# An attention layer's gate in fewer, wider products, spread over two units; two output banks weighted in one operation

## The chip, the cores and the metric

The kernel runs on one core of a Trainium2 chip. The metric is the device time of one execution in microseconds (us). The time before is 621.62 us, the median of 3 runs that lay between 620.19 and 623.57 us.

## The reference

Three layers follow one another, all in float32:

1. Attention with a window: 4 batches, 8 heads, 576 positions, 64 features a head. A position sees itself and the 127 positions before it, with a bias that falls linearly with the distance. The result is 2304 tokens (rows) of 512 features.
2. A first mixture of 8 experts. A token's logits are `x @ w_gate` (8 columns); a ninth column, `x @ w_skip`, says whether the token takes part at all. The expert with the largest logit gets the token: `out = x + gate * relu(x @ w1[e]) @ w2[e]`.
3. A second mixture of 8 experts, in which each expert takes exactly 288 tokens, handed out in the order of the sorted logits. Its logits are 8 more columns of the rows that the first mixture leaves.

Of each finished row of attention the kernel thus needs 17 numbers: 8 logits of the first mixture, the skip score, and 8 logits of the second (which the experts' own output is added to later). In the kernel the 17 columns of weights are one tile, `wcat`, of 128 partitions by 4 chunks of features by 17.

## The kernel before

The 2304 rows are 18 tiles (`t`) of 128 rows. Attention works in **units** `u`: a tile and a half of its heads (`g` = 0 or 1, four heads each), so `u = 2t + g` runs from 0 to 35. The loop over `u` is written out by hand, and every engine executes its instructions in the order in which the code emits them. One pass of the loop holds parts of three units:

- `scores(u)`: 8 products of a query block with 192 keys into two banks of PSUM, `sa` and `sb` (line 196, PE); per head an addition of the bias with the maximum on VectorE (L206), and an exponential on ScalarE (L210), four of each.
- `attend(u - 2)`: the weighted sums over the values, 8 products of half a bank's rows (L247) and 8 of all rows (L253), into two banks `av0` and `av1`; then VectorE multiplies each bank with the reciprocal sums and writes the unit's 256 columns of the row tile `xr[t]` (L257, once for each bank).
- `probs_t(u - 1)`: the probabilities are transposed on PE (L218) and copied to SBUF, `T1` by VectorE (L226) and `T2` by ScalarE (L228).

In every second pass (`g` = 0, from u = 4 on) two more pieces stand around these:

- `gate_x(t - 2)`, ahead of `scores(u)`: the row tile of two tiles ago is transposed on PE (L398, four blocks) and copied by ScalarE to `xt` (L401).
- `gate_l(t - 2)`, behind `attend(u - 2)`: the 17 logits of its 128 rows in 16 small products of 32 rows by 17 columns (`by_quarters`, L410). VectorE copies them (L420, L421), and SP stores the rows to `x2rows` (L422).

A float32 product shows in the trace as two MATMULs and two LDWEIGHTS, so the 16 small products of a tile are 32 and 32 instructions; a transpose shows as one of each.

After a few tiles `gate_l` also appends a generator to `self.steps`: `dispatch` for four tiles (two for the last), `dispatch_one` for the tiles 14 and 15. These choose the expert and the slot of each row and scatter the rows to the experts' slots by GpSimd (POOL). A generator advances one step at each `tick()`, and two while two generators wait; the ticks stand between the VectorE operations of `scores`, `attend` and `probs_t`, nine in a unit. What is left of them is drained behind the loop. Each of them takes one PSUM buffer of the tag `gate`, of which there are two, and which `gate_x`, `gate_l`, `early_gate` and `early_turn` use too.

`early_gate` and `early_turn` (in eight units from u = 15 on) multiply the last two experts' second weights with the second mixture's gate ahead of time (L383, L391). `route_constants` makes constants and is called ahead of the loop; `search_constants` is called at u = 10. `shift_v(t)` copies a tile of values to tiles displaced by 64 rows, on POOL; `attend` reads them. `keep_warm` feeds PE products of zeros in the first microseconds.

Behind the loop come `gate_x` and the logits of tile 16, the last two units, and those of tile 17 inside `layer1`; they keep the 16 small products. `layer1` and `layer2` then run the experts. Nothing of the experts' products can start before the last tile's routing is known.

Of the kernel before, what the change touches and what calls it, by code (L numbers as in the profile page):

```python
# [8 lines left out]
F32 = mybir.dt.float32  # L9
# [3 lines left out]
AF = mybir.ActivationFunctionType  # L13
OP = mybir.AluOpType
AX = mybir.AxisListType

B, H, S, D = 4, 8, 576, 64
# [3 lines left out]
E = 8  # L21
# [17 lines left out]
WARM = (10, 4, 8)  # L39
# [11 lines left out]
class Kernel:  # L51
# [55 lines left out]
    def keep_warm(self, ps, n, name, bufs=1):  # L107

        if not n:
            return  # L110
        p = ps.tile([128, 2, D] if name[:2] == "av" else [128, 4, 128], F32, name=name, bufs=bufs)
        m = p.shape[1] * p.shape[2]
        for _ in range(n):
            self.nc.tensor.matmul(p.rearrange("p h d -> p (h d)"), self.ones, self.zeros[:, :m],
                                  start=True, stop=True)

    def mask_constants(self, pool):

# [27 lines left out]
    def attention(self, debug=None):  # L146
        tc, nc = self.tc, self.nc
# [4 lines left out]
        ps = pool("attps", 1, space=bass.MemoryType.PSUM)  # L152
# [77 lines left out]
        def attend(u):  # L230
            t, g = divmod(u, 2)
            if g == 0:
                self.xr[t] = self.tail.tile([128, SW], F32, name=f"xr{t}") if t in LAST else \
                    self.work.tile([128, SW], F32, name="xr", bufs=9)
                nc.gpsimd.iota(self.xr[t][:, XW:XW + 1], pattern=[[0, 1]], base=128 * t, channel_multiplier=1,
                               allow_small_or_imprecise_dtypes=True)
            av = [ps.tile([128, 2, D], F32, name=f"av{b}") for b in range(2)]
            own, before, mid, early, late = vt[t % NV], vt[max(t - 1, 0) % NV], vs[t % NVS], \
                vs[max(t - 1, 0) % NVS], vs[(t + 1) % NVS]


            for h in range(4):
                r = slice(64 * (h % 2), 64 * (h % 2) + 64)
                small = (own, late) if h % 2 == 0 else (early, before)
                for half in range(2):
                    m = slice(64 * half, 64 * half + 64)
                    nc.tensor.matmul(av[h % 2][m, h // 2], T2[u][r, h // 2, m], small[half][r, 4 * g + h],  # L247
                                     start=(h < 2), stop=False)
            for h in range(4):
                big = (before, mid) if h % 2 == 0 else (mid, own)  # L250
                for half in range(2):
                    m = slice(64 * half, 64 * half + 64)
                    nc.tensor.matmul(av[h % 2][m, h // 2], T1[u][:, h, m], big[half][:, 4 * g + h],  # L253
                                     start=False, stop=(h >= 2))
            x = self.xr[t][:, 256 * g:256 * g + 256].rearrange("p (h b d) -> p h b d", b=2, d=D)
            for b in range(2):
                nc.vector.tensor_tensor(x[:, :, b], av[b], rs[u][:, :, b].to_broadcast([128, 2, D]), op=OP.mult)  # L257
                self.tick()

        self.xr, self.to_slots = {}, []  # L260
# [8 lines left out]
        load_v(1)  # L269
        self.bias_kind(1, 0, 4)  # L270
        self.bias_kind(0, 0, 4)
        self.keep_warm(ps, WARM[1], "av0")
        self.bias_kind(1, 4, 8)
        self.bias_kind(0, 4, 8)
        load_v(2)
# [5 lines left out]
        def gate_l(t):  # L281
            self.gate_l(t)
            if t in ends:
                self.steps.append(self.dispatch(*ends[t]))
            if t in (NT - 4, NT - 3):
                self.steps.append(self.dispatch_one(t, self.lg[:, t]))
# [8 lines left out]
        for u in range(NU):  # L295
            t, g = divmod(u, 2)
            c = t // 2
            if u >= 4 and g == 0:
                self.gate_x(t - 2)
            scores(u)  # L300
            if not u:
                self.keep_warm(ps, WARM[2], "av0")
            if g == 0 and t + 3 < NT:
                load_v(t + 3)
            if g == 0 and t + 1 < NT:
                shift_v(t + 1)
            if u % 4 == 1 and c + 2 < NC:
                load_qk(c + 2)
            if u >= 2:
                attend(u - 2)  # L310
            if u >= 4 and g == 0:
                gate_l(t - 2)
            if u in GATES:
                i = GATES.index(u)
                (self.early_gate, self.early_turn)[i % 2](i // 2)
            if u >= 1:
                probs_t(u - 1)
            if u in LOADS:
                load_w(LOADS.index(u))
            if 3 <= u < 3 + E:  # L320
                first = N * (u - 3)
                nc.sync.dma_start(self.slots[first:first + C1].rearrange("(c n) s -> n c s", c=2),
                                  self.pad[:R1, None, :].to_broadcast([R1, 2, SW]))
            if u == 10:
                self.search_constants()
            if u in (2, 4):
                self.bias_kind(1 + u // 2, 0, 8)
# [21 lines left out]
    def route_constants(self, pool):  # L349

        nc, c = self.nc, self.consts
        self.wcat = c.tile([128, 4, 2 * E + 1], F32, name="wcat")
        nc.sync.dma_start(self.wcat, self.wcat_in)
        self.first = c.tile([128, 1, E], F32, name="first")
        nc.gpsimd.iota(self.first, pattern=[[0, 1], [-1, E]], base=E, channel_multiplier=0,
                       allow_small_or_imprecise_dtypes=True)
        self.base = c.tile([1, 1, E], BF, name="base")
        nc.gpsimd.iota(self.base, pattern=[[0, 1], [N, E]], base=0, channel_multiplier=0,
                       allow_small_or_imprecise_dtypes=True)
        self.w2g = c.tile([128, 16, E], F32, name="w2g")  # L360
        self.count2 = c.tile([128, CAP], F32, name="count2")
        self.count1 = self.count2[:, :C1]
        nc.gpsimd.iota(self.count2, pattern=[[1, CAP]], base=1, channel_multiplier=0,
                       allow_small_or_imprecise_dtypes=True)
        self.lg = c.tile([128, NT, 2 * E + 1], F32, name="lg")
        self.slot = c.tile([128, NT], I32, name="slot")
        self.seen_b = c.tile([128, 1, E], BF, name="seen_b")
        nc.gpsimd.memset(self.seen_b, 0.0)
        pad = pool.tile([128, SW], F32, name="pad")
        nc.gpsimd.memset(pad, 0.0)  # L370
        nc.gpsimd.memset(pad[:, XW:XW + 1], SKIP)
        self.pad = pad
# [32 lines left out]
    def by_quarters(self, p, x, w):  # L405

        for k in range(4):
            for j in range(4):
                m = slice(32 * j, 32 * j + 32)
                self.nc.tensor.matmul(p[m], x[:, k, m], w[:, k], start=(k == 0), stop=(k == 3))  # L410

    def gate_l(self, t):
        nc = self.nc
        p = self.gate_tile([128, 2 * E + 1])
        self.by_quarters(p, self.xt, self.wcat)
        self.keep_l(t, p)

    def keep_l(self, t, p):
# [159 lines left out]
    def layer1(self):  # L578
# [177 lines left out]
        def back(e, c):  # L756
            x2 = self.tail.tile([R1, XW], F32, name=f"xr{LAST[c]}")
            r = slice(R1 * c, R1 * c + R1)
            if e not in EARLY:
                d = ps.tile([R1, E], F32, name="mps", bufs=2)  # L760
                nc.tensor.matmul(d, D[e][:, r], self.pick4, start=True, stop=True)
            p = ps.tile([R1, 4, 128], F32, name="tr", bufs=2)
            for k in range(4):
                nc.tensor.transpose(p[:, k], YT[e][:, k, r], self.ident)
            g = XG[e][c][:, XW + 1:]
            if e in EARLY:
                V.tensor_tensor(x2[:, DM:], D[e][:, c], XG[e][c][:, DM:XW], op=OP.add)
            else:
                V.scalar_tensor_tensor(x2[:, DM:], d, g, XG[e][c][:, DM:XW], op0=OP.mult, op1=OP.add)
            p = p.rearrange("p k d -> p (k d)")  # L770
            if e in EARLY:
                nc.scalar.activation(x2[:, :DM], p, AF.Copy, scale=g)
                nc.gpsimd.tensor_tensor(x2[:, :DM], x2[:, :DM], XG[e][c][:, :DM], op=OP.add)

            if e not in EARLY:
                V.scalar_tensor_tensor(x2[:, :DM], p, g, XG[e][c][:, :DM], op0=OP.mult, op1=OP.add)  # L776
            self.scatter(self.xg_rows, ID[e][:, c:c + 1], x2, stores, N - 1)
# [403 lines left out]
    def search_constants(self):  # L1181
# [5 lines left out]
        self.gate2 = c.tile([128, 4, 32], F32, name="gate2")  # L1187
        nc.gpsimd.memset(self.gate2, 0.0)
        nc.gpsimd.tensor_copy(self.gate2[:, :, :E], self.wcat[:, :, E + 1:])
        self.pick4 = c.tile([128, E], F32, name="pick4")  # L1190
        nc.vector.tensor_reduce(self.pick4, self.ident.rearrange("p (k e) -> p e k", e=32)[:, :E], axis=AX.X, op=OP.add)
        self.step31 = c.tile([128, 31], F32, name="step31")
        nc.gpsimd.iota(self.step31, pattern=[[1, 31]], base=1, channel_multiplier=0, **big)
        self.rows = c.tile([128, 32], BF, name="rows")
# [444 lines left out]
```

## Time and profile before

| | before |
|---|---|
| median of the runs | 621.62 us (620.19 to 623.57) |
| the profiled execution: its own time | 625.05 us |
| its span, first to last instruction | 623.1 us |
| mean granted TensorE clock | 0.983 |
| busy: PE / PE weight loads | 582.6 / 489.8 us |
| busy: VectorE / ScalarE / GpSimd | 292.9 / 265.4 / 270.3 us |

The span and the busy times are of the profiled execution, which took 625.05 us, 1.94 us more than its span. All durations below are from it. PE and PEld are the matmuls and the weight loads of TensorE; their busy times overlap. The names of lines (L196) are those of the code above.

### The profile page before, as it was taken

To read this page: it belongs to the slowest core of one execution; us is meant where nothing else is said; L and a number is where in the kernel's file an instruction comes from. 1 tells how busy PE (TensorE), PEld (TensorE's weight loads), DVE (VectorE), ACT (ScalarE), POOL (GpSimd) and SP (SyncE) were. 2 spreads that over 40 slices of the span, in tenths; PEclk is the share of its full clock that TensorE was granted. 3 is DMA by queue.
4 is the path that set the end of the run, shared out by engine and by line. 5 is a ranking of instruction groups with operands and counts; after the bars stand their busy time and mean duration, and the time that the engine had idled before them with its cause. 6 is when DMAs were issued, how large, how long until landed. Compare 5 with 4: busy or idle time off the path is not lost. (4 is left out here: it accounts for less than half of the span.)

```text
span 623.1 us, 15926 instructions
## 1 busy us (share of the span) xinstructions
PE 582.6 (94%) x6156; PEld 489.8 (79%) x6158; DVE 292.9 (47%) x1331; ACT 265.4 (43%) x826; POOL 270.3 (43%) x354
## 2 busy tenths in 40 slices
PE   7888998987999999999999999999999999999991
PEld 4767777766999999999888767969787878777970
DVE  8876776785110110011136365665656565751320
ACT  4676666761222221222112344536455455455620
POOL 5122314231010110011002465978878787789941
PEclk9999998998999999999999999999999999999996
DMA  8488778531666665666302635353535454583101
GB/s 319 148 269 321 260 271 288 179 131 44 217 210 217 226 238 209 245 238 211 95 1 76 223 140 207 117 172 119 197 137 177 167 175 174 177 327 153 39 2 42
DMA packets 33170, 111.46 MB, mean 179 GB/s; under 512 B 7052, under 2 KB 12172, under 8 KB 24382
## 3 DMA queue, kind: packets, MB, share of 16 engines
q1 hardware_dynamic: 23658, 77.11, 34.9%
q10 hardware_dynamic: 3636, 19.51, 8.4%
q0 software_dynamic: 5792, 13.74, 6.9%
q8 instruction: 50, 0.82, 0.6%
q14 instruction: 34, 0.28, 0.1%
HBM read 93.67 MB, written 20.19 MB: 183 GB/s over the span
## 5 line engine op out<-in xcount | busy, mean ns | idle before, releaser
L552 POOL TENSOR_TENSOR wl<-raw,wh 128x512 fp32r<-128x512 f32 x120 | 152.6, 1297 | 17.5 <-ACT wh L549 15.9
L636 PE MATMUL h<-xt,raw 128*128 128x176 f32 x512 | 86.0, 317 | 0.0
L636 PE MATMUL h<-ht,raw 128*128 128x176 f32 x512 | 81.7, 315 | 0.0
L636 PEld LDWEIGHTS h<-xt,raw 128*128 128x128 f32 x512 | 77.4, 191 | 3.3 <-issue 3.2
L210 ACT ACTIVATE p<-sc,mx 128x192 f32<-128x192 f32 x144 | 63.8, 444 | 32.8 <-DVE mx L206 32.1
L636 PEld LDWEIGHTS h<-ht,raw 128*128 128x128 f32 x512 | 76.7, 190 | 1.0 <-issue 0.7
L549 ACT ACTIVATE wh<-raw 128x512 fp32r<-128x512 f32 x120 | 73.2, 630 | 7.2 <-DVE s_at L1329 3.4
L94 POOL DMA_INDIRECT x2rows<-xr,id x16 | 16.0, 1000 | 125.8 <-DVE xr L776 97.8
L1455 PE MATMUL h<-xh,wh 128*128 128x288 f32 x224 | 68.8, 307 | 0.0
L1457 PE MATMUL h<-xl,wh 128*128 128x288 f32 x224 | 66.3, 296 | 0.0
L1456 PE MATMUL h<-xh,wl 128*128 128x288 f32 x224 | 66.3, 296 | 0.0
L1499 PE MATMUL h<-wh,hh 128*128 128x512 f32 x128 | 53.5, 418 | 0.0
L1499 PE MATMUL h<-wl,hh 128*128 128x512 f32 x128 | 51.7, 404 | 0.0
L1499 PE MATMUL h<-wh,hl 128*128 128x512 f32 x128 | 51.3, 400 | 0.0
L674 ACT ACTIVATE ht<-h 128x176 f32<-128x176 f32 x64 | 20.3, 318 | 70.5 <-PE h L636 67.3
L94 POOL DMA_INDIRECT slots<-xr,slot x18 | 17.9, 997 | 65.8 <-DVE mx L206 31.7
L1477 DVE SCALAR_TENSOR_TENSOR hl<-h,hh 128x288 fp32r<-128x288 f32 x64 | 28.7, 455 | 35.3 <-ACT ht L1476 32.3
L1475 ACT ACTIVATE hh<-h 128x288 fp32r<-128x288 f32 x64 | 26.3, 412 | 42.8 <-PE h L1457 25.0
L1455 PEld LDWEIGHTS h<-xh,wh 128*128 128x128 f32 x224 | 42.4, 189 | 1.3 <-issue 1.0
L1456 PEld LDWEIGHTS h<-xh,wl 128*128 128x128 f32 x224 | 42.2, 188 | 0.2
L1457 PEld LDWEIGHTS h<-xl,wh 128*128 128x128 f32 x224 | 42.1, 188 | 0.0
L1499 PEld LDWEIGHTS h<-wh,hh 128*128 128x128 f32 x128 | 24.0, 187 | 17.5 <-issue 7.5
(322 smaller groups left out, 1164.5 us busy)
## 6 DMA issues: line engine op xcount, KB each, us to landing
raw<-in_moe_w_dram SPq DMA_DIRECT2D x48, 1024.0 KB
raw<-in_moe_w_dram ACTq DMA_DIRECT2D x16, 1024.0 KB
x2rows<-xr SPq DMA_DIRECT2D x18, 260.0 KB
v<-in_v_dram SPq DMA_DIRECT2D x18, 256.0 KB
kt<-in_k_dram SPq DMA_DIRECT2D x8, 512.0 KB
qt<-in_q_dram SPq DMA_DIRECT2D x8, 512.0 KB
raw<-in_moe_w_t_dram SPq DMA_DIRECT2D x4, 1024.0 KB
slots<-pad SPq DMA_DIRECT2D x8, 358.9 KB
```

Source lines behind the costliest of these rows:

```text
L94: st = nc.gpsimd.indirect_dma_start(out=out, out_offset=bass.IndirectOffsetOnAxis(ap=ids, axis=0), in_=rows, in_offset=None, bounds_check= ...
L210: nc.scalar.activation(P[u][:, h], x, AF.Exp, bias=m, scale=-1.0, accum_out=sums[u][:, h:h + 1])
L549: self.lows.append(lambda s=s: nc.scalar.activation(h[:, :, s], x[:, :, s], AF.Copy))
L552: engines[a].tensor_tensor(l[:, :, s], x[:, :, s], h.bitcast(F32)[:, :, s], op=OP.subtract)
L636: nc.tensor.matmul(p, w[:, k, o:o + 128], x[:, k], start=first, stop=last)
L674: nc.scalar.activation(HT[e][:, f], p, AF.Relu)
L1455: nc.tensor.matmul(p, wh, xh, start=first, stop=False)
L1456: nc.tensor.matmul(p, wl, xh, start=False, stop=False)
L1457: nc.tensor.matmul(p, wh, xl, start=False, stop=last)
L1475: nc.scalar.activation(hh[:, f], p, AF.Relu)
L1477: after(1, lambda f=f, p=p: V.scalar_tensor_tensor(hl[:, f], p, 0.0, hh.bitcast(F32)[:, f], op0=OP.max, op1=OP.subtract))
L1499: nc.tensor.matmul(p, x[i][:, 4 * g + f, a:a + 128], w[j][:, f], start=(s + f + g == 0), stop=(s == 2 and f == 3 and g == 1))
```

## The change

The 17 logits of a tile come in three steps now:

1. `gate_x(t - 2)` stands behind `scores(u)` of the even pass instead of ahead of it.
2. `gate_m`, new, stands ahead of `scores(u + 1)`, in the odd pass: four products, one for each chunk of features, of a zero-padded copy of the weights (`wide`, 32 columns) with `xt`, each into its own 32 partitions of a 128 x 128 tile. ScalarE copies that tile to `gate_s`.
3. `gate_l`, behind `scores(u + 1)`: one product of `gate_s` with a constant of ones (`pick4`, now 17 columns wide) adds the four chunks up and turns them at once. The copies, the store and the new generators follow it as before, so they come in the odd pass.

`wide` and `pick4` are made in `route_constants`, ahead of the loop (`pick4` was made in `search_constants`). `av0` and `av1` become one tile of two banks, and one VectorE operation weights both; the two ticks follow it.

```diff
+        if name == "av":
+            p = ps.tile([128, 2, 512], F32, name=name, bufs=bufs)[:, 0, :2 * D]
...
-            av = [ps.tile([128, 2, D], F32, name=f"av{b}") for b in range(2)]
+            av = ps.tile([128, 2, 512], F32, name="av")[:, :, :2 * D].rearrange("p b (h d) -> p b h d", d=D)
...
-            for b in range(2):
-                nc.vector.tensor_tensor(x[:, :, b], av[b], rs[u][:, :, b].to_broadcast([128, 2, D]), op=OP.mult)
+            nc.vector.tensor_tensor(x, av.rearrange("p b h d -> p h b d"), rs[u].to_broadcast([128, 2, 2, D]), op=OP.mult)
+            for _ in range(2):
                 self.tick()
...
-            if u >= 4 and g == 0:
-                self.gate_x(t - 2)
+            if u >= 4 and g:
+                self.gate_m()
             scores(u)
+            if u >= 4:
+                gate_l(t - 2) if g else self.gate_x(t - 2)
...
             if u >= 2:
                 attend(u - 2)
-            if u >= 4 and g == 0:
-                gate_l(t - 2)
...
         nc.sync.dma_start(self.wcat, self.wcat_in)
+        self.wide = c.tile([128, 4, 32], F32, name="wide")
+        nc.gpsimd.memset(self.wide, 0.0)
+        nc.gpsimd.tensor_copy(self.wide[:, :, :2 * E + 1], self.wcat)
+        self.pick4 = c.tile([128, 2 * E + 1], F32, name="pick4")
+        nc.vector.tensor_reduce(self.pick4, self.ident.rearrange("p (k e) -> p e k", e=32)[:, :2 * E + 1], axis=AX.X,
+                                op=OP.add)
...
+    def gate_m(self):
+
+        p = self.gate_tile([128, 128])
+        for k in range(4):
+            self.nc.tensor.matmul(p[32 * k:32 * k + 32], self.wide[:, k], self.xt[:, k], start=True, stop=True)
+        self.gate_s = self.work.tile([128, 128], F32, name="gate_s")
+        self.nc.scalar.activation(self.gate_s, p, AF.Copy)
+
     def gate_l(self, t):
...
-        self.by_quarters(p, self.xt, self.wcat)
+        self.nc.tensor.matmul(p, self.gate_s, self.pick4, start=True, stop=True)
         self.keep_l(t, p)
...
-                nc.tensor.matmul(d, D[e][:, r], self.pick4, start=True, stop=True)
+                nc.tensor.matmul(d, D[e][:, r], self.pick4[:, :E], start=True, stop=True)
```

## Rows read from the trace of the kernel before

**Rows 1.** Windows, loop from u = 4: us, then each engine's busy us, granted clock, DMA.

```profile
19.53:136.23 116.70, 104.31 (x2402) 84.79 (x2401) 88.55 (x519) 78.80 (x309) 33.46 (x90) 0.99 0.71 245
```

**Rows 2.** Timeline of PE: start, us, engine, line (first and last unit, one tile).

```profile
19.53 0.38 PE L196 MATMUL sa<-kt,qt 64*64 64x192 f32 x2
...
102.23 0.60 PE L398 MATMUL gate<-ident,xr 128*128 128x128 f32 x4
102.76 0.38 PE L196 MATMUL sa<-kt,qt 64*64 64x192 f32 x2
...
103.46 0.22 PE L247 MATMUL av<-v,t 64*64 64x64 f32 x1
...
104.42 0.45 PE L410 MATMUL gate<-wcat,xt 128*32 128x17 f32 x32
104.80 0.87 PE L218 MATMUL pt<-ident,p 128*128 128x128 f32 x6
105.60 0.38 PE L196 MATMUL sa<-kt,qt 64*64 64x192 f32 x2
...
136.23 0.38 PE L196 MATMUL sa<-kt,qt 64*64 64x192 f32 x2
```

**Rows 3.** Timeline of the same tile: VectorE, ScalarE, and what PE waits for.

```profile
103.79 0.36 DVE L206 CUSTOM_DVE_ANT_0 sc<-sa,bias 128x192 f32<-128x192 f32 x1 [0.52 <-PE sb L196]
...
105.52 0.44 ACT L210 ACTIVATE p<-sc,mx 128x192 f32<-128x192 f32 x1
...
106.80 0.37 ACT L228 ACTIVATE t<-pt 128x256 f32<-128x256 f32 x1
...
107.22 0.27 PE L247 MATMUL av<-v,t 64*64 64x64 f32 x1 [0.74 <-ACT t L228]
```

**Rows 4.** Groups by line, loop from u = 4: busy us, mean ns | idle before, releaser.

```profile
L410 PEld LDWEIGHTS gate<-wcat,xt 128*32 128x32 f32 x512 | 7.3, 111 | 7.1 <-issue 6.1
L398 PEld LDWEIGHTS gate<-ident,xr 128*128 128x128 f32 x60 | 6.9, 141 | 2.2 <-DVE xr L257 1.8 <-issue 0.2
L247 PE MATMUL av<-v,t 64*64 64x64 f32 x248 | 14.2, 224 | 3.0 <-ACT t L228 2.5 <-issue 0.5
L383 PE MATMUL gate<-raw,gate 128*32 128x128 f32 x128 | 4.3, 276 | 0.0
```

**Rows 5.** Windows: the stretch behind three pauses of L410.

```profile
97.57:100.00 2.43, 2.43 (x21) 1.93 (x22) 1.37 (x7) 0.38 (x1) 0.94 (x3) 0.50 0.72 188
```

**Rows 6.** Groups by line, same loop, ScalarE and VectorE: the nearest operations.

```profile
L401 ACT ACTIVATE xt<-gate 128x512 f32<-128x512 f32 x16 | 9.4, 589 | 1.5 <-PE gate L398 0.5 <-PE sb L196 0.3
L386 ACT ACTIVATE gate_t<-gate 128x128 f32<-128x128 f32 x4 | 1.1, 265 | 1.6 <-PE gate L383 1.6
L257 DVE TENSOR_TENSOR xr<-av,rs 128x128 f32<-128x128 f32 x62 | 15.3, 284 | 5.2 <-POOL w L176 1.9 <-remote 1.8 <-PE av L253 1.4
L226 DVE COPY t<-pt 128x512 f32<-128x512 f32 x31 | 21.0, 676 | 6.5 <-PE pt L218 4.9 <-PE sb L196 1.5
```

**Rows 7.** The page's part on DMA queues: the two kinds of instruction loads.

```profile
q8 instruction: 50, 0.82, 0.6%
```

**Rows 8.** Timeline of the start: POOL, SP's queue, and the first weighted sum on PE.

```profile
2.24 0.20 POOL L355 IOTA first<- 128x8 f32 x1
...
4.38 0.44 SPq L353 DMA_DIRECT2D wcat<-in_w_cat_dram  x1
...
6.67 0.60 POOL L176 COPY w<-v 64x512 f32<-64x512 f32 x1 [3.15 <-DMA v<-in_v_dram]
...
7.91 0.62 POOL L179 COPY w<-v 64x512 f32<-64x512 f32 x1
10.11 0.61 POOL L176 COPY w<-v 64x512 f32<-64x512 f32 x1 [1.58 <-DMA v<-in_v_dram]
...
13.21 0.27 PE L247 MATMUL av<-v,t 64*64 64x64 f32 x1 [0.37 <-ACT t L228]
```

**Rows 9.** Timeline behind the loop: POOL's scatter of tile 15.

```profile
142.88 0.97 POOL L94 DMA_INDIRECT slots<-xr,slot  x1 [2.33 <-DVE mx L490]
```

More of the change, by code (lines that the diff above doesn't have):

```diff
@@ L110, in keep_warm @@
             return
-        p = ps.tile([128, 2, D] if name[:2] == "av" else [128, 4, 128], F32, name=name, bufs=bufs)
-        m = p.shape[1] * p.shape[2]
+        if name == "av":
+            p = ps.tile([128, 2, 512], F32, name=name, bufs=bufs)[:, 0, :2 * D]
+        else:
+            p = ps.tile([128, 4, 128], F32, name=name, bufs=bufs).rearrange("p h d -> p (h d)")
         for _ in range(n):
-            self.nc.tensor.matmul(p.rearrange("p h d -> p (h d)"), self.ones, self.zeros[:, :m],
-                                  start=True, stop=True)
+            self.nc.tensor.matmul(p, self.ones, self.zeros[:, :p.shape[1]], start=True, stop=True)
     def mask_constants(self, pool):
@@ L246, in attend @@
                     m = slice(64 * half, 64 * half + 64)
-                    nc.tensor.matmul(av[h % 2][m, h // 2], T2[u][r, h // 2, m], small[half][r, 4 * g + h],
+                    nc.tensor.matmul(av[m, h % 2, h // 2], T2[u][r, h // 2, m], small[half][r, 4 * g + h],
                                      start=(h < 2), stop=False)
@@ L252, in attend @@
                     m = slice(64 * half, 64 * half + 64)
-                    nc.tensor.matmul(av[h % 2][m, h // 2], T1[u][:, h, m], big[half][:, 4 * g + h],
+                    nc.tensor.matmul(av[m, h % 2, h // 2], T1[u][:, h, m], big[half][:, 4 * g + h],
                                      start=False, stop=(h >= 2))
             x = self.xr[t][:, 256 * g:256 * g + 256].rearrange("p (h b d) -> p h b d", b=2, d=D)
-            for b in range(2):
-                nc.vector.tensor_tensor(x[:, :, b], av[b], rs[u][:, :, b].to_broadcast([128, 2, D]), op=OP.mult)
+            nc.vector.tensor_tensor(x, av.rearrange("p b h d -> p h b d"), rs[u].to_broadcast([128, 2, 2, D]), op=OP.mult)
+            for _ in range(2):
                 self.tick()
@@ L271, in attention @@
         self.bias_kind(0, 0, 4)
-        self.keep_warm(ps, WARM[1], "av0")
+        self.keep_warm(ps, WARM[1], "av")
         self.bias_kind(1, 4, 8)
@@ L297, in attention @@
             c = t // 2
-            if u >= 4 and g == 0:
-                self.gate_x(t - 2)
+            if u >= 4 and g:
+                self.gate_m()
             scores(u)
+            if u >= 4:
+                gate_l(t - 2) if g else self.gate_x(t - 2)
             if not u:
-                self.keep_warm(ps, WARM[2], "av0")
+                self.keep_warm(ps, WARM[2], "av")
             if g == 0 and t + 3 < NT:
@@ L410, in by_quarters @@
                 self.nc.tensor.matmul(p[m], x[:, k, m], w[:, k], start=(k == 0), stop=(k == 3))
+    def gate_m(self):
[4 more added lines that the diff above has]
+        self.nc.scalar.activation(self.gate_s, p, AF.Copy)
     def gate_l(self, t):
-        nc = self.nc
         p = self.gate_tile([128, 2 * E + 1])
-        self.by_quarters(p, self.xt, self.wcat)
+        self.nc.tensor.matmul(p, self.gate_s, self.pick4, start=True, stop=True)
         self.keep_l(t, p)
@@ L1189, in search_constants @@
         nc.gpsimd.tensor_copy(self.gate2[:, :, :E], self.wcat[:, :, E + 1:])
-        self.pick4 = c.tile([128, E], F32, name="pick4")
-        nc.vector.tensor_reduce(self.pick4, self.ident.rearrange("p (k e) -> p e k", e=32)[:, :E], axis=AX.X, op=OP.add)
         self.step31 = c.tile([128, 31], F32, name="step31")
```

## Prediction

> **What bounds the kernel now.** I read the page first: behind attention PE is busy without a break up to the end, so whatever the change is worth must be worth it in the attention loop, and comes through one to one as an earlier or later start of the experts. Then I read the windows. The loop from u = 4 takes 116.70 us for 31 units (first and last scores at 19.53 and 136.23), 3.76 us a unit or 7.53 a tile, and in it PE is busy for 104.31, VectorE for 88.55, ScalarE for 78.80 [rows 1, 2]. PE is the fullest, but no engine is full, so I read the timeline of one tile for what PE's order costs without any stall.
>
> In the even unit: scores 0.70 (102.76 to 103.46), the weighted sums 0.96, the 16 gate products 0.38, the transposes 0.80 (104.80 to 105.60), together 2.84. The odd unit has `gate_x` (0.53, 102.23 to 102.76) in place of the gate products: 0.70 + 0.96 + 0.80 + 0.53 = 2.99 [rows 2]. A tile's floor is 5.83, 15.5 tiles make 90.4, and the loop lies 26.3 us above that. The view of groups says where a good part of it is: weight loads of L410 idle for 6.1 with nothing to wait for ("issue"); 2.5 are waits of the weighted sums for ScalarE's copy `T2`; 1.8 are waits of `gate_x` for the row tile; the early gate's own products take 4.3 [rows 4]. [...]
>
> **What the change adds on the path.** The copy `xt` now comes, in ScalarE's order, behind the four exponentials of `scores(u)`, and `gate_m` must have it before PE may start `scores(u + 1)`. That makes one serial chain, priced from this tile. From the start of scores, the first VectorE operation is at +1.03 and the fourth exponential starts at +2.76 and ends at +3.20 [rows 3]. The copy takes 0.59 [rows 6] and PE starts 0.05 after a ScalarE copy that it waits for (107.17 to 107.22) [rows 3]: +3.84. PE itself arrives at 0.70 + 0.53 + 0.96 + 0.80 = +2.99, and so stands for 0.85 in each tile. Behind `gate_m` nothing of PE can pass: `scores(u + 1)` is queued there, and VectorE and ScalarE wait for it in turn.
>
> `gate_m` is four products, 8 instructions, of the early gate's shape (32 columns of weights, 128 moving): 128 of those kept PE busy for 4.3 us [rows 4], 8 of them 0.27. I take 0.25, as they overlap. The odd unit's scores thus start at +4.09, where they now start at +2.84.
>
> The odd unit loses `gate_x` and gains one product of 17 columns. Its bounds are 0.02 (two of L410's 32 instructions in 0.38) and 0.13 (a block of `gate_x`) [rows 2]; I take 0.07: 0.70 + 0.07 + 0.96 + 0.80 = 2.53. `gate_s` costs nothing: ScalarE does it in 0.265 [rows 6] while PE does the 0.70 of scores; without that cover it would be 0.3 a tile. The tile's floor becomes 4.09 + 2.53 = 6.62, or 102.6 for 15.5 tiles: **12.2 us more than now.**
>
> **What it takes away.** Not much work: PE's own sum goes from 5.83 to 5.77. What goes are stalls. First the pauses in L410, 6.1, and the half clock behind them, 1.2. Only the small products pause like that: the early gate's 128 instructions have an idle of 0.0, L410's 512 one of 7.1 [rows 4]. The waits for `T2` go (2.5), as the odd unit's weighted sums now come at +4.09 + 0.77 and `T2`, behind `xt`, is done at +3.79 + 0.37. The waits of `gate_x` for the row tile go too (1.8), because it moves behind 0.70 of scores. Together 11.6. Of the remaining 14.7, the 4.3 of the early gate stay. Of the 10.4, what falls behind the scores of an even unit hides in PE's 0.85 of slack, up to 13 us in all. Dispatch's products for instance now land behind the even unit's transposes, by their count of ticks. The bounds are 0 and about half, 5.2; I take a quarter, 2.6.
>
> The trace has 50 loads on the queue of instructions, 0.82 MB, 16.4 KB each [rows 7]. [...] If the pauses are no loads of instructions, fewer instructions need not end them; that is a rival below.
>
> **Edits off the path.** The merged operation weights 256 columns at once. Two of 128 keep VectorE busy for 15.3 / 62 x 2 = 0.49; one of 256 lies between 0.284 (128) and 0.676 (a copy of 512) [rows 6]; a straight line gives 0.41. The 0.08 are hidden behind PE (VectorE is busy for 88.55 of 116.70 [rows 1]), so I take 0, with up to 1.2 where the denser odd units leave VectorE no room (15.5 x 0.08). It waits for all 16 products instead of 14, which end together.
>
> At the start there are two costs. `pick4` now stands on VectorE ahead of the first scores: at most one operation of 0.28 [rows 6], I take 0.2. On POOL the copy to `wide` waits for `wcat`, and the constants, then `shift_v(0)`, are queued behind it. `wcat` is issued behind two tiles of `v` on the same queue; the first of these landed at 10.1 [rows 8], so some 0.8 later is my estimate for `wcat`. POOL's work from 2.24 to 8.53 is 3.1 without its wait of 3.15, so `shift_v(0)` ends near 14.3 instead of 8.53. The first weighted sum, at 13.21 [rows 8], reads it: about 1.1 late, of which I expect 0.3 to reach the loop, where the first units wait for each other anyway. Bounds 0 and 1.1.
>
> At the end the generators start a unit later, and more of tile 15's steps are drained behind the loop. The scatter of tile 15 (142.88) [rows 9] must be down before the first rows are loaded for the experts. VectorE's last passes get about 0.8 of generator steps more, and lose most of it again as fewer steps stand between the maxima: +0.2, between -0.5 and +0.9.
>
> **Sum.** Loop: +12.2 - 11.6 - 2.6 = -2.0. Start +0.5, end +0.2. In all -1.3 us of the profiled 625.05, that is 623.75; the runs' median stands 0.55% below the profiled execution, so 620.3. That is not to be told from no change: a difference within 0.5% (3.1 us) I count as none.
>
> **Rivals.**
>
> *The slack absorbs more (faster).* The even half hides all that it can, 5.2 instead of 2.6, and the odd half's VectorE gains its 1.2: -5.1, which gives 616.6. For it: PE gets 0.85 us to breathe in each tile, and 22 fewer instruction pairs of 144. Against it: pauses ahead of the last exponential delay the new chain one to one. It is faster by over 0.5% once 4.4 of the 10.4 go. Chance 0.28.
>
> *The pauses stay (slower).* They belong to the stream and not to the small products, and strike other groups. Then of 7.3 (6.1 and 1.2) some 5.5 come back, the rest hides in the even half: +4.2, which gives 625.8. It decides from 4.4 us on. For it: other groups pause too. Against it: the 0.0 of the early gate. Chance 0.22.
>
> *The clock falls (slower).* PE now stands in each tile. The only drop in the loop followed three pauses in one group; the cost was 1.2 for 2.43 us [rows 5]. If five of the 16 waits end like that, +6.0, in all +4.7: 626.3. [...] Against it: the waits of 0.74 for `T2` [rows 3] were of the same length and the loop's mean clock is 0.99 [rows 1]. Chance 0.07.
>
> **The numbers.** My forecast, a new wait that eats what the stalls give back, has 0.43 and gives 620.3; its own range is 617.5 to 623.5. The first rival is faster, the two others are slower; with the forecast's edges that makes 0.30 faster, 0.41 no difference, 0.29 slower. The range for 8 in 10 goes from 615.0 (the first rival's 616.6, less half of the 2.5 that the clock and the pauses of other groups leave open) to 626.5 (the slower two).
>
> **What would show it.** Scores of an odd unit start about 4.1 after those of the even unit, and an even unit's about 2.5 to 2.9 after the odd one's. The weight loads of `gate_m` wait for `xt` for 0.8 to 0.9 in most tiles, 12 to 14 us in all. The waits for `T2` and of `gate_x` for the row tile are gone, and idles that end in "issue" fall by more than 5. The merged operation takes 0.41, the first weighted sum starts near 14.3, and the loop's clock stays at 0.99. I am wrong if `xt` is ready when PE arrives (then the kernel is faster by some ten us, 15.5 x 0.85 less what else comes up), or if "issue" stays where it was.

## The result: slower by 1.2%

| | before | after |
|---|---|---|
| median of runs | 622.32 us (620.19 to 623.57, 4 runs) | 629.3 us (628.82 to 631.29, 4 runs) |
| profiled execution, its span | 625.05, 623.1 | 628.82, 626.7 |
| scores of u = 4 | 19.53 | 20.07 |
| loop, first to last scores | 116.70 | 120.05 |
| last scores to the experts' first product | 21.26 | 21.41 |
| from there to the end | 465.56 | 465.16 |

The ratio is 1.0122, 95% interval 1.0084 to 1.0159. Timed again beside other runs of the kernel before, it was 1.0176 (1.0118 to 1.0234). Runs more than 1.5% above the fastest of their kernel are left out of the ratios, so a ratio need not be the quotient of the two medians given. The loop pays +3.4 us of the profiled execution's +3.8, the start +0.5, the end of attention +0.15, and the experts take 0.4 less. So the loop is the place to look.

The windows of the changed kernel give the loop as one row; it answers to [rows 1]:

```profile
20.07:140.12 120.05, 110.04 (x2050) 82.37 (x2050) 88.27 (x488) 82.64 (x329) 32.91 (x91) 1.00 0.67 233
```

PE has 352 matmul instructions fewer, 22 for each of 16 tiles, and yet more busy time, and the clock is full. One tile in PE's timeline, with its weight loads (PEld) and what stands on ScalarE and VectorE, answers to [rows 2, 3]:

```profile
31.63 0.38 PE L197 MATMUL sa<-kt,qt 64*64 64x192 f32 x2
...
32.44 0.30 PEld L430 LDWEIGHTS gate<-pick,gate_s 128*128 128x128 f32 x2 [0.28 <-issue]
32.44 0.40 PE L430 MATMUL gate<-pick,gate_s 128*128 128x17 f32 x2
...
32.77 0.27 PE L248 MATMUL av<-v,t 64*64 64x64 f32 x1
...
34.58 0.38 PE L197 MATMUL sa<-kt,qt 64*64 64x192 f32 x2
35.39 0.42 PEld L405 LDWEIGHTS gate<-ident,xr 128*128 128x128 f32 x4 [0.28 <-issue]
35.39 0.65 PE L405 MATMUL gate<-ident,xr 128*128 128x128 f32 x4
35.60 0.36 DVE L207 CUSTOM_DVE_ANT_0 sc<-sa,bias 128x192 f32<-128x192 f32 x1 [0.23 <-PE sb L197]
...
36.98 0.88 PE L219 MATMUL pt<-ident,p 128*128 128x128 f32 x6
37.34 0.44 ACT L211 ACTIVATE p<-sc,mx 128x192 f32<-128x192 f32 x1
37.78 0.57 ACT L408 ACTIVATE xt<-gate 128x512 f32<-128x512 f32 x1
38.40 0.43 PE L423 MATMUL gate<-xt,wide 128*32 128x128 f32 x8 [0.54 <-ACT xt L408]
...
38.76 0.38 PE L197 MATMUL sa<-kt,qt 64*64 64x192 f32 x2
```

Read the even unit from 34.58. VectorE starts at +1.02, the fourth exponential at +2.76, `xt` at +3.20; `gate_m` (L423) waits for it until +3.82, and the odd unit's scores start at +4.18. PE could have started `gate_m` 0.80 after its transposes, at 37.78, so it loses 0.62. The odd unit, from 31.63 to 34.58, takes 2.95. In it `gate_l` (L430) starts 0.81 behind the start of scores, where the weighted sums of before come at 0.70 [rows 2], and the sums follow 0.33 later. Its weight load, and that of `gate_x` (L405), stands still for 0.28 with nothing to wait for.

The groups of the loop say how often; the two figures behind the bar are busy time and mean, then idle time. They answer to [rows 4, 6]:

```profile
L257 DVE TENSOR_TENSOR xr<-av,rs 128x256 f32<-128x256 f32 x32 | 13.4, 419 | 10.4 <-PE pt L219 4.0 <-POOL w L177 3.0 <-PE av L254 2.2
...
L248 PE MATMUL av<-v,t 64*64 64x64 f32 x248 | 14.6, 230 | 0.0
L405 PEld LDWEIGHTS gate<-ident,xr 128*128 128x128 f32 x64 | 6.7, 141 | 4.5 <-issue 2.0 <-DVE t L227 2.0 <-DVE rs L223 0.3
L430 PEld LDWEIGHTS gate<-pick,gate_s 128*128 128x128 f32 x30 | 4.5, 188 | 4.2 <-issue 3.6 <-ACT gate_s L425 0.6
L423 PEld LDWEIGHTS gate<-xt,wide 128*32 128x32 f32 x128 | 2.6, 107 | 11.3 <-ACT xt L408 11.3
```

11.3 us of idle weight loads in 16 tiles end in `xt`. The waits of L248's products for `T2`, 2.5 before, are gone, and so are the 6.1 of L410. But `gate_x` and the new `gate_l` have idles that the old order didn't have: 4.5 in 16 tiles (`gate_x` had 2.2, nearly all waits for the row tile) and 4.2 in 15, 0.28 each. The trace of before showed such an idle too, in dispatch's four loads behind the scores, 1.1 in all:

```profile
L452 PEld LDWEIGHTS <-upto 128*128 128x128 bf16 x4 | 0.4, 96 | 1.1 <-issue 1.1
```

The start, from the timelines of POOL and PE, and the end, as [rows 8]:

```profile
11.48 0.24 POOL L357 COPY wide<-wcat 128x68 f32<-128x68 f32 x1 [8.94 <-DMA wcat<-in_w_cat_dram]
...
14.25 0.27 PE L248 MATMUL av<-w,t 64*64 64x64 f32 x2 [0.33 <-POOL w L178]
...
161.53 0.42 PE L651 MATMUL h<-xt,raw 128*128 128x176 f32 x1
```

POOL stood for 8.94 until `wcat` was there. The weighted sums began at 13.50 instead of 13.21, and the first that reads POOL's shifted rows waited for them until 14.25.

### The profile page after: what moved, and what is told of

Same layout as the page of the kernel before. It is cut to its first block, busy times and chain, and to the rows that moved or that the text cites. A ratio compares the mean times of both kernels' runs of the same rounds, so it can differ in the third digit from the quotient of the medians.

```text
span 626.7 us, 15218 instructions
## 1 busy us (share of the span) xinstructions
PE 591.6 (94%) x5806; PEld 489.0 (78%) x5806; DVE 292.7 (47%) x1295; ACT 267.8 (43%) x842; POOL 270.5 (43%) x356
## 5 line engine op out<-in xcount | busy, mean ns | idle before, releaser
L1488 ACT ACTIVATE hh<-h 128x288 fp32r<-128x288 f32 x64 | 26.3, 411 | 43.1 <-PE h L1470 23.7
```

The costliest lines, as they stand in the source:

```text
L1488: nc.scalar.activation(hh[:, f], p, AF.Relu)
```

## The experiments

Times are medians. Beside the experiments before took 618.4 us (19 runs), 618.88 (17) and 616.65 (17): one figure for each group of kernels that shared a chip, here the first four, the next four and the last three experiments. Loops are from the first to the last scores of the profiled execution.

**`gate_x` back in its old place, the rest of the change kept.**

```diff
-            if u >= 4 and g:
-                self.gate_m()
+            if u >= 4:
+                self.gate_m() if g else self.gate_x(t - 2)
             scores(u)
-            if u >= 4:
-                gate_l(t - 2) if g else self.gate_x(t - 2)
+            if u >= 4 and g:
+                gate_l(t - 2)
```

> The changed kernel, but gate_x stands ahead of the even unit's scores again, as before the change. If the wait of gate_m for xt is what the change pays with: that wait (0.7 us in each of 16 tiles) goes, and the tile's floor falls from 7.13 to 6.27 (even 0.70 + 1.01 + 0.80 + 0.35, odd 0.82 + 0.32 + 1.01 + 0.73 + 0.53): 13 us less than the changed kernel, about 616. If another wait takes its place (T2 for the odd unit's sums) or the pauses return: 621 to 629.

616.23 us (10 runs), ratio 0.9992 (0.9953 to 1.0031). Two units in PE's timeline:

```profile
28.48 0.38 PE L197 MATMUL sa<-kt,qt 64*64 64x192 f32 x2
...
30.95 0.43 PE L423 MATMUL gate<-xt,wide 128*32 128x128 f32 x8
31.30 0.38 PE L197 MATMUL sa<-kt,qt 64*64 64x192 f32 x2
...
34.83 0.38 PE L197 MATMUL sa<-kt,qt 64*64 64x192 f32 x2
```

The even unit takes 2.82 instead of 4.18, and `gate_m` waits for nothing; the odd one takes 3.53, as `gate_x` is back in it. 6.35 a tile against 7.13 is 12.1 us in 15.5 tiles; the loop fell by 13.5 (106.51). The median is 11.6 and 13.1 us below the changed kernel's two (627.85 and 629.3), the ratio lower by 8 to 11 us' worth. So the place of `gate_x` is what makes the change slow: with it undone, the rest comes out even with before.

**`gate_l` behind the odd unit's transposes, the rest as changed.**

```diff
-                gate_l(t - 2) if g else self.gate_x(t - 2)
+            if u >= 4 and not g:
+                self.gate_x(t - 2)
 ...
                 probs_t(u - 1)
+            if u >= 4 and g:
+                gate_l(t - 2)
```

> The changed kernel, but gate_l (its one product, the copies and the store) stands behind the odd unit's transposes instead of behind its scores. If its 0.44 us are the price of a product on the whole array between products on quarters of it: 0.34 less a tile, 5 us in all, about 624. If they are the price of its two loads of 128 columns wherever it stands: no change, 629.

In PE's timeline of an odd unit the product now has the next scores close behind it:

```profile
121.02 0.38 PE L197 MATMUL sa<-kt,qt 64*64 64x192 f32 x2
...
122.68 0.87 PE L219 MATMUL pt<-ident,p 128*128 128x128 f32 x6
123.39 0.29 PE L432 MATMUL gate<-pick,gate_s 128*128 128x17 f32 x2
123.61 0.38 PE L197 MATMUL sa<-kt,qt 64*64 64x192 f32 x2
```

From the transposes to the scores there are 0.93 instead of 0.80: here the product costs 0.13. Odd units without other work take 2.59 instead of 2.95, and the loop 114.94 instead of 120.05, as expected (a second profile of the changed kernel has 117.75). The time didn't follow: 627.28 (624.2 to 629.82, 4 runs), ratio 1.0177 (1.0116 to 1.0238), the changed kernel's own. The profiled execution (624.2) is the fastest of the four. What the others lost isn't in the trace and stays open.

**The 16 old products in the place of `gate_m`,** with neither `gate_s` nor the single product; their order against `xt` is the changed one.

```diff
 def gate_l(self, t):
-        self.nc.tensor.matmul(p, self.gate_s, self.pick4, start=True, stop=True)
+        self.by_quarters(p, self.xt, self.wcat)
 ...
             if u >= 4 and g:
-                self.gate_m()
+                gate_l(t - 2)
             scores(u)
-            if u >= 4:
-                gate_l(t - 2) if g else self.gate_x(t - 2)
+            if u >= 4 and not g:
+                self.gate_x(t - 2)
```

> The changed kernel's order with the old 16 small products in gate_m's place, and no gate_s, no single product. It has the same wait for xt. Its floor is 3.83 + 0.38 for the even and 2.51 for the odd unit, 6.72 for 7.13. If the pauses came from the stream or from chance and are gone anyway: 6 us less than the changed kernel, about 623. If the pauses belong to the small products: they come back, with 5 to 7 us, and it is near 629; the weight loads of the small products then idle for 5 us or more with nothing to wait for.

625.58 us (4 runs), ratio 1.0153 (1.009 to 1.0216): slower without any of the new products, by the order and its wait. The group of the small products, and one odd unit, which has no gate product at all:

```profile
L417 PEld LDWEIGHTS gate<-wcat,xt 128*32 128x32 f32 x512 | 5.6, 112 | 11.1 <-ACT xt L408 11.1
```

```profile
24.27 0.38 PE L197 MATMUL sa<-kt,qt 64*64 64x192 f32 x2
...
25.93 0.88 PE L219 MATMUL pt<-ident,p 128*128 128x128 f32 x6
26.73 0.38 PE L197 MATMUL sa<-kt,qt 64*64 64x192 f32 x2
```

The small products wait for `xt` and have no pause of the kind that [rows 4] showed; PE pauses 4.0 us in all at other groups. The odd unit takes 2.46: beside it, `gate_l` costs 0.49 where the change put it (2.95) and 0.13 behind the transposes (2.59).

**The merged weighting alone,** in the order of before (the second half of the change).

```diff
-            for b in range(2):
-                nc.vector.tensor_tensor(x[:, :, b], av[b], rs[u][:, :, b].to_broadcast([128, 2, D]), op=OP.mult)
+            nc.vector.tensor_tensor(x, av.rearrange("p b h d -> p h b d"), rs[u].to_broadcast([128, 2, 2, D]), op=OP.mult)
```

> The kernel before with one part of the change alone: both banks weighted in one operation. If VectorE's 0.08 a unit are hidden behind PE, as I forecast: no change, 622 within 1.5. If VectorE ends the odd units: up to 2.9 less.

620.66 us (613.84 to 626.35, 10 runs), ratio 1.0019 (0.9972 to 1.0066): no difference, as the prediction had it.

**The kernel before, profiled once more.** No edit.

> The kernel before, unchanged, profiled once more. If the pauses of TensorE that the trace of before showed with nothing waited for (10.0 us in the loop, 5.9 of them at L410) belong to the kernel, they are there again, 9 to 11 us, and the profiled execution takes 624 to 626 us. If they differ from execution to execution, their sum is another one, 2 to 9 us, and the loop (116.70) is shorter by about as much.

Its group of small products, and below it that of the version with the merged weighting, which has the same 512:

```profile
L410 PEld LDWEIGHTS gate<-wcat,xt 128*32 128x32 f32 x512 | 5.7, 112 | 2.2 <-issue 1.2
```

```profile
L411 PEld LDWEIGHTS gate<-wcat,xt 128*32 128x32 f32 x512 | 5.7, 112 | 1.7 <-issue 0.7
```

1.2 and 0.7, where [rows 4] have 6.1. Yet the loop of the second profile is hardly shorter (115.67), as the view of waits and its window tell:

```profile
PE av L253 <- issue: 2.3, 1, 2.3
PE av L247 <- issue: 1.8, 2, 1.0
```

```profile
20.32:135.99 115.67, 104.32 (x2401) 85.37 (x2400) 87.41 (x515) 77.73 (x308) 33.40 (x90) 0.96 0.70 246
```

PE's own idles with nothing waited for are 7.4 us in this loop, against 7.8 in the first profile and 3.8 in the one with the merged weighting, whose loop takes 108.0. They moved, from L410 to L253 and L247, and the clock was at half for about 9 us here (an estimate from the window's mean of 0.96), 3.4 in the first profile. So the pauses of the first profile were no mishap of that execution as a sum; their place was. The execution took 621.21, against 625.05, and 2.9 of these 3.8 us lie in the end of attention (18.3 instead of 21.3).

What half the clock costs, PE's timeline of the first profile shows in the stretch of [rows 5]: the transposes take 1.47 there (0.80 in the tile of [rows 2]), the scores 1.34 (0.70).

```profile
97.56 1.54 PE L218 MATMUL pt<-ident,p 128*128 128x128 f32 x6
99.03 0.59 PE L196 MATMUL sa<-kt,qt 64*64 64x192 f32 x2
...
100.37 0.31 PE L247 MATMUL av<-v,t 64*64 64x64 f32 x1
```

**`gate_l`'s product issued twice.** The second writes the same result.

```diff
-        self.nc.tensor.matmul(p, self.gate_s, self.pick4, start=True, stop=True)
+        for _ in range(2):
+            self.nc.tensor.matmul(p, self.gate_s, self.pick4, start=True, stop=True)
```

> The changed kernel with the single product of gate_l issued twice in a row, the second writing the same result. If what made it 0.44 instead of 0.07 is the step from quarter-array products to whole-array ones and back, the second costs 0.05 to 0.10 and the odd unit, 2.95 unhindered, takes 3.00 to 3.05; time 628 to 632. If the product itself, with its weight load, is that dear, the odd unit takes 3.27 to 3.40, and the time rises by 5 to 7 us.

PE's timeline in an odd unit:

```profile
77.14 0.38 PE L197 MATMUL sa<-kt,qt 64*64 64x192 f32 x2
...
77.95 0.62 PE L431 MATMUL gate<-pick,gate_s 128*128 128x17 f32 x4
78.50 0.27 PE L248 MATMUL av<-v,t 64*64 64x64 f32 x1
```

Neither theory was right alone. From scores to the sums it takes 1.36 instead of 1.14: the second product costs 0.22, and unhindered odd units take 3.17. So of the first one's 0.44 up to the sums, 0.22 is what a repetition costs, and the other 0.22 belong to its place between scores and sums: it starts 0.11 later than sums would (0.81 for 0.70), and the sums come another 0.11 late. Its first load stands for 0.28 there, partly behind products that still run. The one execution took 631.82.

**The two constants made at the fourth unit.** `wide` and `pick4` are computed when u is 3 instead of ahead of the loop.

```diff
+            if u == 3:
+                self.gate_constants()
             if u == 10:
                 self.search_constants()
```

> The changed kernel with its two new constants made when the loop is at its fourth unit, not ahead of the loop. If they delay the loop's start, the start of the scores of unit 4 falls from 20.07 to about 19.5 and the time by 0.5 us; if something else does, it stays at 20.0 to 20.1.

The loop's first scores in PE's timeline:

```profile
19.61 0.51 PE L197 MATMUL sa<-kt,qt 64*64 64x192 f32 x3 [1.09 <-issue]
```

19.61 instead of 20.07. One pair doesn't show that the 0.5 is theirs: the two profiles of before start at 19.53 and 20.32, and the next version, with the constants late too, at 20.18. Over all profiles the loop starts at 19.81 to 21.97 in the seven with constants ahead (median 20.07) and at 19.11 to 20.32 in the six without (19.57). So 0.5 fits the medians, and single executions differ by more. What is clear of the spread is the first sum that reads the shifted rows: 13.98 to 14.38 with the constants ahead, 12.87 to 13.72 without. The one execution took 630.25 all the same, as the end took 24.3 instead of 21.4; that is the clock, below.

**All three: `gate_x` back, `gate_l` late, constants late.**

```diff
+            if u >= 4:
+                self.gate_m() if g else self.gate_x(t - 2)
             scores(u)
-            if u >= 4:
-                gate_l(t - 2) if g else self.gate_x(t - 2)
 ...
                 probs_t(u - 1)
+            if u >= 4 and g:
+                gate_l(t - 2)
 ...
+            if u == 3:
+                self.gate_constants()
```

> The changed kernel with gate_x back ahead of the even unit's scores, gate_l's product behind the odd unit's transposes, and the two constants made at the fourth unit. By the prices read so far a tile is 0.70 + 1.01 + 0.80 + 0.35 = 2.86 even and 0.70 + 1.01 + 0.73 + 0.10 + 0.53 = 3.07 odd, 5.93 in all against 6.27 with only gate_x back: 5 us less over 15.5 tiles, so 611 (608 to 614), 0.987 of before. If instead gate_l's late place makes VectorE's keep_l end after the next gates want it, the gain goes and the time is 615 to 618.

617.85 us (616.04 to 622.02, 12 runs), ratio 0.9991 (0.9959 to 1.0023): 611 is missed, and the second figure, 615 to 618, holds. The floor did fall: 2.82 and 3.22 in the first units. Then PE came too early for VectorE, as in this unit, and the windows have a stretch of half clock:

```profile
77.99 0.66 DVE L227 COPY t<-pt 128x512 f32<-128x512 f32 x1
...
78.70 0.27 PE L254 MATMUL av<-v,t 128*64 128x64 f32 x1 [0.65 <-DVE t L227]
```

```profile
110.40:117.20 6.80, 6.39 (x64) 4.97 (x61) 3.79 (x26) 3.45 (x14) 0.24 (x1) 0.50 0.10 39
```

The copy `t` had come behind dispatch's steps on VectorE, the last of which started at 77.58. The loop took 110.15: 16.5 above its floor of 15.5 x 6.04, where the version with `gate_x` back alone is 8.1 above 98.4. 3.2 of it is the half clock, an estimate: half of PE's 6.39. PE's own waits for VectorE and ScalarE are 5.2 in this loop, against 1.5 in that version: 2.1 for `t`, 1.8 for `gate_l`'s copy into `xr`, which the expectation named, and 1.3 for a copy of the early gate. The rest of the difference isn't taken apart.

**`gate_m` behind the odd unit's scores, `gate_l` behind its transposes,** with `gate_x` where the change put it.

```diff
-            if u >= 4 and g:
-                self.gate_m()
             scores(u)
             if u >= 4:
-                gate_l(t - 2) if g else self.gate_x(t - 2)
+                self.gate_m() if g else self.gate_x(t - 2)
 ...
                 probs_t(u - 1)
+            if u >= 4 and g:
+                gate_l(t - 2)
```

> The changed kernel with gate_x where the change put it, but gate_m behind the odd unit's scores, so that ScalarE copies xt under these, and gate_l behind the odd unit's transposes. If the wait for xt is what the even unit pays, it falls from 4.18 to 3.20 (1.42 from the transposes to gate_m and 0.36 from there to the scores become 0.80), the odd unit is 2.59 + 0.35 = 2.94, and by 15.5 tiles of 6.14 instead of 7.13 the loop loses 15 us: 105, time 614. If VectorE and ScalarE are then late, as with the tile of 5.89, it loses 8 to 10: 618 to 620.

626.01 us (4 runs), ratio 1.0132 (1.0083 to 1.0182): both figures missed. The even unit is 3.21, as expected. The odd one is 3.83 instead of 2.94, in the timelines of PE and ScalarE:

```profile
99.54 0.38 PE L197 MATMUL sa<-kt,qt 64*64 64x192 f32 x2
...
102.30 0.44 ACT L211 ACTIVATE p<-sc,mx 128x192 f32<-128x192 f32 x1
...
102.73 0.25 ACT L425 ACTIVATE gate_s<-gate 128x128 f32<-128x128 f32 x1
...
103.04 0.40 PE L430 MATMUL gate<-pick,gate_s 128*128 128x17 f32 x2 [0.34 <-ACT gate_s L425]
...
103.37 0.38 PE L197 MATMUL sa<-kt,qt 64*64 64x192 f32 x2
```

It is the same chain once more: now `gate_s` stands behind four exponentials, at +3.19, and PE waits for it ahead of the next scores. The wait wasn't removed, it moved from `xt` to `gate_s`.

**`gate_x` back and constants late, `gate_l` as changed.**

```diff
+            if u >= 4:
+                self.gate_m() if g else self.gate_x(t - 2)
             scores(u)
-            if u >= 4:
-                gate_l(t - 2) if g else self.gate_x(t - 2)
+            if u >= 4 and g:
+                gate_l(t - 2)
 ...
+            if u == 3:
+                self.gate_constants()
```

> The changed kernel with gate_x back ahead of the even unit's scores, and the two constants made at the fourth unit. The tile stays at 2.82 + 3.53 = 6.35; the loop starts at about 19.6 instead of 21.97 if the constants made it late there, of which the loop's length takes back some: 615 (613 to 617), 0.995 of before. If that late start was a mishap of one execution, the time is that of the version with gate_x back alone, 616 to 617, ratio 0.998 to 1.000.

614.48 us (610.64 to 619.23, 12 runs), ratio 0.9959 (0.9932 to 0.9987): the only version that is faster than before, by 0.4%, less than the 0.5% that I count as a difference. Its loop starts at 19.11 and takes 105.63.

**The changed kernel once more.** No edit.

> The changed kernel, unchanged, timed once more beside more runs of the kernel before. If the result of 1.012 holds, it is 1.010 to 1.018 of before again, with 15 waits of gate_m for the ACT copy of xt, 0.54 each, and 1.5 to 4 us of pauses with nothing waited for. If the loss belonged to those first runs, the ratio falls under 1.006.

627.85 us (4 runs), ratio 1.0176 (1.0118 to 1.0234), loop 117.75. The result stands.

## Why the prediction was wrong

The mechanism, the chain over `xt`, was right. Two sizes were wrong, and both made the forecast too low.

- **The chain over `xt`: right.** VectorE at +1.02 (1.03 predicted), fourth exponential +2.76 (2.76), end of `xt` +3.77 (3.79), `gate_m` +3.82 (3.84). The two runs that keep this order in other forms (the old small products, `gate_l` late) are slower by 1.5 and 1.8%, and with `gate_x` back the ratio is 0.999.
- **`gate_l` at 0.07: wrong, the first step that failed.** I took its price, and the bounds of 0.02 and 0.13, from two neighbours and didn't ask what stands on either side of it. It costs 0.49: 0.44 up to the sums and 0.05 in them. 0.22 is the price of a repetition, 0.27 that of its place between the scores and the sums. Behind the transposes it costs 0.13. That the step between products of quarters and of the whole array makes the price fits this, but no run changed the shapes alone. `gate_m` was 0.36 instead of 0.25. The floor is 4.18 + 2.95 = 7.13 instead of 6.62: +0.51, or 7.9 us in 15.5 tiles, of which `gate_l` is 6.5.
- **`gate_x` behind scores: 0.70 instead of 0.53,** but it stands in PE's slack; so the wait is 0.62 instead of 0.85, and the end doesn't change.
- **The rest above the floor: 2.6 better than predicted.** 120.05 - 15.5 x 7.13 = 9.5, where I had left 12.1. The first rival had these 2.6, but they aren't enough for it. 7.9 - 2.6 = 5.3 is the miss of the loop (+3.4 instead of -2.0). The second profile of the changed kernel has the same floor and 2.3 less above it. My odd unit of before, 2.99, was put together from the even unit's parts; where nothing holds it, it takes 3.05 in both profiles, so 0.9 of the 26.3 above the floor were floor.
- **From the profiled execution to the median: wrong, the second step that failed.** I took 0.55% off, as before's profiled execution stood above its runs, while after's stands 0.5 us below its median. That is 3.9 us, and with 5.1 between the profiled times (628.82 and 623.75) the miss of 9.0. Before's profiled execution, 625.05, is above all other timed runs of that kernel, and all that the change was to take away was read from it alone.
- **The pauses of L410: gone as forecast, but not as a property of these products.** PE's idles with nothing waited for fell from 7.8 us in the loop to 2.6. In the second profile of before they are 7.4, of which L410 has 1.1. How much of them, and of the half clock, a typical execution of before has to give back stays open. The 1.2 for the half clock was my estimate, half of the 2.43 us of [rows 5]; the stretch in the loop is 3.4 us long in the first profile, so by the same estimate it cost 1.7.
- **"Only the small products pause like that": refuted** as to the place, by the same products elsewhere without pauses, and by pauses at other groups. But the sum goes with them: 3.8 to 7.8 us in the four profiles whose kernels have the 512 small instructions, 0 to 2.6 in the nine others. Whether it is these products or the number of instructions isn't shown. The rival that the pauses stay isn't borne out; what came in L405 and L430 comes in every tile, by the place of the product.
- **The clock falls: didn't happen** in the loop, which had 1.00 with 16 waits for `xt`, 8.0 us in all.
- **Off the path: right, in part by luck.** Merged weighting 0.419 (0.41), and no difference by itself; waits for `T2` gone; the shifted rows read at 14.25 (14.3, though the sums began at 13.50 with others). Start +0.54 (+0.5) and end +0.15 (+0.2) are luck in a single pair: two profiles of before differ by 0.8 in the start and by 2.9 in the end.

Of my own signs, the even unit's scores at 2.95 behind the odd one's, not 2.5 to 2.9, was the one that told of the first error. The sign on "issue" depends on where one looks: PE's idles fell by 5.2, those of the weight loads only from 14.7 to 13.5, as the stands of `gate_x` and `gate_l` came in.

## What to carry to other kernels

Price a TensorE instruction at its place: look in the trace of before for the gap between two neighbours of the same two shapes (whole array behind quarters, quarters behind whole; that the shapes alone make the gap is not shown), not for the busy time of a like instruction somewhere else. Here it was there: dispatch's L452 starts 0.81 to 0.82 behind the start of the scores, as `gate_l` does now at 0.81. Before a copy is put behind a unit's exponentials on an engine that ran them in the order of the code, as ScalarE did here (fourth exponential at +2.76, `xt` at +3.20), add up when it can be ready at the earliest, and put its reader behind that; moving the reader alone only moved the wait. A pause with nothing waited for is put down to an instruction only when a second profile shows it at the same place; what the pauses sum to wants several profiles.

## What I had not expected of the hardware

- **Whole-array weight loads behind the scores stand for 0.28 with nothing to wait for** (L405, L430; 4.5 and 4.2 us in the loop; L452 before), and in the place behind the transposes `gate_x` had none of that (2.2 in 60 loads, 1.8 of it waits [rows 4]). `gate_m`'s loads, 128 rows by 32 columns, stood for 4.5 in 15 tiles when they were put there, 0.30 each, though the profile puts these down to ScalarE's copies (4.0 to `xt`, 0.6 to `T2`). Part of L405's 4.5 is put down to VectorE's `t`, but in the version with the old small products the same 4.5 had no releaser at all:

```profile
L405 PEld LDWEIGHTS gate<-ident,xr 128*128 128x128 f32 x64 | 6.7, 140 | 4.5 <-issue 4.5
```

- **Pauses move.** The two profiles of before have them at different groups; L410 had 6.1 and 1.2. The queue of instruction loads, which I had in view in [rows 7], went from 50 to 48 with the change (51 with the old products in the new place):

```profile
q8 instruction: 48, 0.79, 0.5%
```

No run here shows that a load caused a pause, so the cause stays open.
- **The end of attention runs in part at half clock (granted 0.50), for a time that changes from execution to execution.** In the two profiles of before, stretches of 6.8 and 3.4 us at half clock begin in it, and it takes 21.3 and 18.3 us. Windows of three other kernels (the changed one, the one with constants late, and the fastest version), each of the stretch at half clock behind the loop:

```profile
147.20:157.40 10.20, 9.24 (x131) 7.74 (x121) 4.53 (x26) 0.97 (x3) 1.14 (x3) 0.50 0.19 60
```

```profile
146.80:163.00 16.20, 14.93 (x116) 12.97 (x116) 5.89 (x39) 1.65 (x5) 2.90 (x7) 0.50 0.21 70
```

```profile
131.10:134.50 3.40, 3.40 (x72) 3.09 (x73) 2.55 (x20) 0.42 (x2) 1.23 (x5) 0.50 0.17 63
```

From the last scores to the experts' first product these took 21.4, 24.3 and 18.7. 5.6 us between these executions from this stretch alone are more than most effects in this study, and one reason why single times (631.82, 630.25) say little here. What PE had done before the clock fell was alike: busy for 4.56 of 7.08 us, 5.67 of 8.10 and 4.38 of 6.36.
